# Weight groups narrowed in stages, one stage a step, in a two-MLP kernel on one core

## The chip, the cores and the metric

The kernel runs on one core of one Trainium2 chip. The metric is the device time of one execution in microseconds; the median of several executions is given. The engines are called as the profile calls them: PE (TensorE, matrix products; PEld is its loading of weights), DVE (VectorE), ACT (ScalarE), POOL (GpSimd) and SP (SyncE, which issues the transfers here).

## The reference

A Fourier transform over sequence and features, its real part, and then two MLPs one after the other, with float32 results:

```python
def _attn_ref(x):                      # x: 2 x 3008 x 256
    X = np.fft.fft(x, axis=1)
    X = np.fft.fft(X, axis=2)
    return X.real.astype(np.float32)

def _moe_ref(x, w_in, w_out):          # 6016 x 256, 256 x 2048, 2048 x 256
    r = np.maximum(x @ w_in, 0.0)
    return ((r * r) @ w_out).astype(np.float32)

def _moe2_ref(x, w_in, w_out):
    h = x @ w_in
    g = h * (1.0 / (1.0 + np.exp(-1.702 * h)))
    return (g @ w_out).astype(np.float32)
```

The weights come as float64. They reach the chip as pairs of 32-bit words, and the kernel makes float32 of them itself.

## The kernel before

**Products.** Every float32 operand of a product is held as a high part of a rounded type and a low part, the rest. A product of two operands is three matrix products: high with high, high with low, low with high. The tokens are cut into eight blocks of 376 or 378 columns (two halves each, which the symmetry of the transform ties together).

**Steps.** The first MLP is one loop of 128 steps (L684 to L737), numbered from 0. A step takes one block j and one slice f of 128 hidden features. PE makes the hidden product into a pair of banks of PSUM (`front1`, L453 to L455; two such pairs exist, so PE is at most two steps ahead of DVE), then the output product of the step that lies four steps back (`back`, L468, `LAG = 4`). DVE evacuates the hidden product with three instructions (L710, L712, L713), the last of which frees the second bank. ACT does relu, square and the high part (L719, L720, L722); in the steps of the set `SV` DVE does relu and square in one instruction (L717). POOL subtracts for the low part (L76, tile gl); in the steps of `VSTEPS` DVE does. Where a block ends, `store` (L573) copies the two output sums from PSUM, one on ACT and one on DVE (L581), and sends them to DRAM.

**Background work.** Everything else that the two MLPs need is a generator of items, an item being mostly one instruction. `PLAN` (L33) gives for each generator the first step, the rate in items per step, and the step by which it must be done. `background(i)` (L558) takes the items that fall on step i. The scheduler of the language orders each engine's instructions by the order in which they are written and by when it expects them to be ready; from step 18 on (`THROTTLE`) a DVE or ACT instruction of the background stands behind that step's last DVE or ACT instruction. A generator that isn't done at its due step is run to its end there.

**Narrowing.** `narrow` (L162) makes float32 of a group of weights, 1024 per partition, in six items: Abs of the high words on ACT (L169), a clamp of the result (L170) and a shift (L171) on DVE, the scaled low words (on ACT, L175, for the groups in the set `RA`, else on DVE, L177), the merging of sign and top bit (L178) and the addition (L180), both on DVE. L171 reads L170's result, L178 that of L175 or L177, L180 those of L171 and L178. Then the group is widened into a high part (a copy on ACT, L203 or L241) and a low part (a subtraction, L76, tile w or w2i, on POOL or DVE by the table `LOW`). The input groups of the first MLP have a sum and a masked difference between the two (L200, L201), those of the second four differences on POOL (L233), two copies and two subtractions, each in two instructions.

**Where it runs.** A group is named by MLP, kind (0 input, 1 output) and number. "conv" narrows groups (0,0,1), (0,1,1), (0,0,2), (0,1,2), (0,0,3), (0,1,3) from step 3 on; the scratch tiles of the kinds differ. "w2a" narrows (1,0,2), (1,1,2), (1,0,3) from step 55, "w2b" (1,1,3), (1,0,0), (1,1,0), (1,0,1), (1,1,1) from step 85; all groups of these two share one scratch tile, so the Abs of a group waits for the last subtraction of the group before. `then` loads the next group's words by SP once `narrow` is done; `park` (L211) sends four of the widened w2 groups to DRAM until they are needed. "odd1" (`odd_k`, L398) prepares two blocks of the second batch from step 79: two sums, then for each block `split_eo` (high part on ACT, low part on POOL for the first and DVE for the second) and `nyquist`, a small matrix product (L418, L419) that reads both parts.

The second MLP follows the loop, in an order written out by hand. It doesn't concern the change.

Of the kernel before, what the change touches and what calls it, by code (L numbers as in the profile page):

```python
# [12 lines left out]
AF = mybir.ActivationFunctionType  # L13
# [19 lines left out]
PLAN = {  # L33
# [4 lines left out]
}  # L38
# [25 lines left out]
def spectral_two_mlps_kernel(  # L64
# [7 lines left out]
    def f32(ap):  # L72
        return ap.bitcast(F32)
# [88 lines left out]
    def narrow(raw, ue, key=None):  # L162
# [5 lines left out]

        yield lambda: A.activation(out=u, in_=f32(hw), func=AF.Abs)  # L169
        yield lambda: V.tensor_scalar(out=u, in0=u, scalar1=LEAST, scalar2=TOP, op0=ALU.max, op1=ALU.min)  # L170
        yield lambda: V.tensor_scalar(out=uu, in0=uu, scalar1=3, scalar2=0x3FFFFFF8,  # L171
                                      op0=ALU.logical_shift_left, op1=ALU.bitwise_and)

        if key in RA:
            yield lambda: A.activation(out=eu, in_=lw, func=AF.Copy, scale=2.0 ** -29)  # L175
        else:
            yield lambda: V.tensor_scalar(out=eu, in0=lw, scalar1=2.0 ** -29, scalar2=None, op0=ALU.mult)  # L177
# [4 lines left out]
    def temp(pool, tag="xt"):  # L182
        return pool.tile([P, 2, 1024], F32, tag=tag, name="ue")
# [3 lines left out]
    def widen(mlp, kind, g, temps, dest, then=None, tag="xt"):  # L187
# [17 lines left out]
        if mlp and (kind, g) in PARKED:  # L205
            park((mlp, kind, g), w)
        weights[mlp, kind, g] = w

    parked = {}
# [188 lines left out]
    def odd_k(b, pool, tag="xt", later=0):  # L398
# [26 lines left out]
        yield lambda: sums(1)  # L425
        yield lambda: split_eo(b, 2, e2)
        yield lambda: nyquist(2)
        while at_step[0] < later:
            yield lambda: None
        yield lambda: split_eo(b, 3, e3)  # L430
        yield lambda: nyquist(3)

# [95 lines left out]
    def at(name, job):  # L528
        i, rate, end = PLAN[name]
        plan.setdefault(i, []).append((name, rate, job))  # L530
        if end is not None:
# [5 lines left out]
    at("conv", lambda: chain(*(  # L537
        widen(0, k, g, xp, (winp, wq)[k], tag=("t", "x0")[k],
              then=(lambda k=k, g=g: load_w(0, k, g + 1)) if g < 3 else None)
        for g in (1, 2, 3) for k in range(2))))  # L540
# [101 lines left out]
    def w2_jobs(lo, hi):  # L642
        for i in range(lo, hi):
# [3 lines left out]
            if k == 0:  # L647
                yield from widen_in(g, temp(cv2), dest, then=then)
            else:
                yield from widen(1, 1, g, cv2, dest, then=then)  # L650

# [347 lines left out]
```

## Time and profile before

| | |
|---|---|
| median of 3 runs | 1035.78 us (1034.14 to 1037.46) |
| the profiled execution | 1034.19 us, span of its instructions 1032.1 us |
| PE busy | 987.3 us, 96% of the span |
| DVE, ACT, POOL busy | 823.0, 616.4, 351.0 us |
| mean granted clock of PE | 0.985 |
| the 128 steps of the first MLP | from about 35 to 520 us |
| PE busy from 524 us to the end | 503.5 of 508.1 us |

The profile is one execution. Busy times of a stretch come from the table by windows; an instruction's start and duration from the timeline, where the bracket at the end of a line is the time for which its engine was idle before it and what ended that. A granted clock of 1.00 is 2.4 GHz, 0.50 is 1.2 GHz. The busy time of PE is that at whichever clock was granted.

### The profile page before, as it was taken

The numbers are of one execution on the slowest core, as the hardware profiler recorded it, in microseconds if no ns is written. First come the engines' busy times: TensorE is split into PE (matmuls) and PEld (weight loads), VectorE is DVE, ScalarE is ACT, GpSimd is POOL, SyncE is SP. The second block draws the span as 40 slices with busy tenths as digits, with TensorE's granted clock in tenths as the row PEclk, the third lists the DMA queues.
The fourth block names the chain that finished last, engine by engine and source line by source line (L and its number), as shares of the span: only waits on it lengthen the run. The fifth ranks groups of instructions, "written<-read, shape, count | busy, mean of one in ns | idle before, by whom it ended". The sixth has DMA issues, their size and how long they took to land.

```text
span 1032.1 us, 14239 instructions
## 1 busy us (share of the span) xinstructions
PE 987.3 (96%) x5582; PEld 951.4 (92%) x5582; DVE 823.0 (80%) x1089; ACT 616.4 (60%) x764; POOL 351.0 (34%) x216
## 2 busy tenths in 40 slices
PE   8988988999989999898989999999999999999998
PEld 8578987898989799898989999999999999999997
DVE  7997889885877579677668888888988888888875
ACT  2576576775688578787754554554555455454443
POOL 2457474534567546776715210102020020200000
PEclk9898999999999999999999999999999999999999
DMA  7532212101142112101342100000100000000000
GB/s 286 209 108 80 72 71 82 72 31 53 42 140 85 72 67 88 70 32 61 114 138 94 61 31 30 30 32 7 54 1 30 31 31 31 1 31 1 31 1 30
DMA packets 22914, 65.22 MB, mean 63 GB/s; under 512 B 1856, under 2 KB 14272, under 8 KB 19648
## 3 DMA queue, kind: packets, MB, share of 16 engines
q1 hardware_dynamic: 22848, 64.32, 17.5%
q8 instruction: 43, 0.70, 0.3%
q14 instruction: 23, 0.19, 0.1%
HBM read 43.13 MB, written 21.19 MB: 62 GB/s over the span
## 4 chain that ended last, share of the span: by engine, by line
PE 53%; DVE 3%; ACT 2%; issue 1%; POOL 0%; DVEq 0%; ACTq 0%
PE psb L779 25%; PE psc L763 22%; PE psb L468 4%; ACT h L720 1%; ACT h L719 1%; PE psa L453 1%; PE psa L455 0%; PE psa L454 0%; DVE ue L177 0%; DVE gl L76 0%; DVE ue L178 0%; DVE ue L170 0%; ACT gh L722 0%; DVE yc L76 0%; DVE h L712 0%
## 5 line engine op out<-in xcount | busy, mean ns | idle before, releaser
L76 POOL TENSOR_TENSOR gl<-h,gh 128x752 fp32r<-128x752 f32 (+1 forms) x113 | 215.3, 1913 | 170.8 <-ACT gh L722 153.3
L468 PE MATMUL psb<-gh,w 128*128 128x376 f32 (+1 forms) x1024 | 244.4, 341 | 4.0 <-ACT o L581 3.4
L779 PE MATMUL psb<-gh,w 128*128 128x376 f32 (+1 forms) x1024 | 237.7, 334 | 0.0
L468 PEld LDWEIGHTS psb<-gh,w 128*128 128x128 f32 x1024 | 187.2, 193 | 5.5 <-ACT o L581 4.5
L779 PEld LDWEIGHTS psb<-gh,w 128*128 128x128 f32 x1024 | 182.9, 188 | 0.0
L719 ACT ACTIVATE h<-h 128x752 f32<-128x752 f32 (+1 forms) x116 | 96.5, 832 | 79.5 <-DVE h L713 77.3
L844 ACT ACTIVATE g<-c 128x1128 f32<-128x1128 f32 (+1 forms) x64 | 73.8, 1152 | 99.7 <-DVE c L842 99.7
L468 PE MATMUL psb<-gl,w 128*128 128x376 f32 (+1 forms) x512 | 133.1, 341 | 0.0
L779 PE MATMUL psb<-gl,w 128*128 128x376 f32 (+1 forms) x512 | 129.9, 335 | 0.4 <-DVE gl L76 0.3
L722 ACT CAST gh<-h 128x752 fp32r<-128x752 f32 (+1 forms) x128 | 105.3, 822 | 22.7 <-DVE h L717 19.5
L453 PE MATMUL psa<-eo,w 128*128 128x376 f32 (+1 forms) x256 | 90.3, 354 | 25.1 <-DVE h L713 15.1
L76 DVE TENSOR_TENSOR gl<-g,gh 128x1504 fp32r<-128x1504 f32 (+1 forms) x64 | 111.7, 1745 | 1.6 <-ACT gh L824 1.6
L824 ACT CAST gh<-g 128x1504 fp32r<-128x1504 f32 (+1 forms) x64 | 93.1, 1454 | 31.8 <-DVE g L815 31.8
L710 DVE SCALAR_TENSOR_TENSOR p<-n,w1n_t,psa 128x376 f32<-128x376 f32 (+1 forms) x128 | 75.9, 599 | 45.0 <-PE psa L455 44.9
L615 POOL TENSOR_TENSOR ue<-raw 128x376 f32<-128x376 f32 (+1 forms) x16 | 19.5, 1237 | 270.6 <-DVE ya L76 270.5
L720 ACT ACTIVATE h<-h 128x752 f32<-128x752 f32 (+1 forms) x116 | 96.7, 835 | 3.3
L468 PEld LDWEIGHTS psb<-gl,w 128*128 128x128 f32 x512 | 95.5, 194 | 0.0
L779 PEld LDWEIGHTS psb<-gl,w 128*128 128x128 f32 x512 | 92.1, 188 | 1.0 <-DVE gl L76 1.0
L815 DVE TENSOR_TENSOR g<-g,c 128x1128 f32<-128x1128 f32 (+1 forms) x64 | 89.5, 1399 | 1.2 <-ACT g L844 1.2
L841 DVE TENSOR_TENSOR g<-g,psc 128x376 f32<-128x376 f32 (+1 forms) x64 | 35.0, 546 | 68.9 <-ACT g L840 68.9
L454 PE MATMUL psa<-eo,w 128*128 128x376 f32 (+1 forms) x256 | 86.2, 337 | 0.0
L455 PE MATMUL psa<-eo,w 128*128 128x376 f32 (+1 forms) x256 | 86.1, 337 | 0.0
(138 smaller groups left out, 1627.8 us busy)
## 6 DMA issues: line engine op xcount, KB each, us to landing
ydram<-o SPq DMA_DIRECT2D x18, 376.0 KB, 2.8
xt<-in_x SPq DMA_DIRECT2D x5, 1024.0 KB, 7.0
cst<-in_dfts SPq DMA_DIRECT2D x8, 570.0 KB, 6.0
raw<-ydram SPq DMA_DIRECT2D x6, 752.0 KB, 4.6
out<-o SPq DMA_DIRECT2D x11, 376.0 KB, 3.1
raw<-in_w1i SPq DMA_DIRECT2D x4, 1024.0 KB, 5.8
raw<-in_w1o SPq DMA_DIRECT2D x4, 1024.0 KB, 7.3
raw<-in_w2i SPq DMA_DIRECT2D x4, 1024.0 KB, 4.9
```

The source lines that it names most:

```text
L76: eng.tensor_tensor(out=o, in0=a, in1=f32(b), op=ALU.subtract)
L453: T.matmul(o, lhsT=w[:, 0, fs], rhs=t[:, par, 0, 0:wd], start=True, stop=False)
L454: T.matmul(o, lhsT=w[:, 0, fs], rhs=t[:, par, 1, 0:wd], start=False, stop=False)
L455: T.matmul(o, lhsT=w[:, 1, fs], rhs=t[:, par, 0, 0:wd], start=False, stop=True)
L468: T.matmul(acc[j][ec][:, s, 0:wd], lhsT=w[:, hl, e0:e0 + P], rhs=(gh, gl)[gi][:, s, 0:wd], start=(first and hl == 0 and gi == 0), stop=(la ...
L719: A.activation(out=hv, in_=hv, func=AF.Relu)
L720: A.activation(out=hv, in_=hv, func=AF.Square)
L722: last_a = A.copy(gh[:, :, 0:wd], hv)
L763: T.matmul(bank, lhsT=w[:, hl, slot * P:(slot + 1) * P], rhs=t[:, yl, i], start=(first and hl == 0 and yl == 0), stop=(hl == 1), skip_grou ...
L779: T.matmul(o[:, s, 0:wd], lhsT=w[:, hl, e0:e0 + P], rhs=g[:, 2 * i + s, 0:wd], start=(f == 0 and hl == 0 and g is gh), stop=(f == 15 and h ...
L815: V.tensor_tensor(out=g[:, 1:4, 0:pw], in0=g[:, 1:4, 0:pw], in1=c[:, :, 0:pw], op=ALU.mult)
L824: A.copy(gh[:, :, 0:pw], g[:, :, 0:pw])
```

## The change

The items of a group are handed out in stages. `staged` draws several items of a group's generator at once: for a group in `RA` two, two and two of `narrow` (Abs and scaled low words on ACT; clamp and shift on DVE; merging and addition on DVE), for another one, three and two (Abs; clamp, shift and scaled low words on DVE; merging and addition). Then follow, for an output group, the copy and the subtraction, one a stage; for an input group of the first MLP, sum and masked difference, the copy, the subtraction; for one of the second, the four differences, the first copy, the first subtraction with the second copy, the second subtraction. For the groups in `RA`, except the very first one, the scaled low words come right behind Abs. The rates go from 2, 1.6 and 1.7 items to 1.2, 1 and 1.04 stages a step; first and due steps stay. In w2, an empty item follows a group whose low part POOL makes, unless it is the last of its generator. In "odd1" an empty item stands between `split_eo` and `nyquist`.

```diff
-    "out0": (0, 12, 3), "even01": (0, 1, 4), "odd0": (1, 1, 48), "conv": (3, 2, 36),
+    "out0": (0, 12, 3), "even01": (0, 1, 4), "odd0": (1, 1, 48), "conv": (3, 1.2, 36),
...
-    "cst3": (66, 4, 67), "odd1": (79, 1, 88), "w2a": (55, 1.6, 78), "w2b": (85, 1.7, 117), "y0": (117, 1, 128),
+    "cst3": (66, 4, 67), "odd1": (79, 1, 88), "w2a": (55, 1, 78), "w2b": (85, 1.04, 117), "y0": (117, 1, 128),
...
         yield lambda: A.activation(out=u, in_=f32(hw), func=AF.Abs)
+        early = key in RA and key != (0, 0, 0)
+        if early:
+            yield lambda: A.activation(out=eu, in_=lw, func=AF.Copy, scale=2.0 ** -29)
...
-        if key in RA:
+        if early:
+            pass
+        elif key in RA:
             yield lambda: A.activation(out=eu, in_=lw, func=AF.Copy, scale=2.0 ** -29)
...
+    def staged(key, gen):
+
+        mlp, kind, _ = key
+        first = (2, 2, 2) if key in RA else (1, 3, 2)
+        for k in first + ((1,) if kind else (4, 1, 2) if mlp else (2, 1)):
+            yield lambda: run(gen, k)
+        yield lambda: run(gen)
...
         yield lambda: split_eo(b, 2, e2)
+        yield from [lambda: None] * b
         yield lambda: nyquist(2)
...
         yield lambda: split_eo(b, 3, e3)
+        yield from [lambda: None] * b
         yield lambda: nyquist(3)
...
-        widen(0, k, g, xp, (winp, wq)[k], tag=("t", "x0")[k],
-              then=(lambda k=k, g=g: load_w(0, k, g + 1)) if g < 3 else None)
+        staged((0, k, g), widen(0, k, g, xp, (winp, wq)[k], tag=("t", "x0")[k],
+                                then=(lambda k=k, g=g: load_w(0, k, g + 1)) if g < 3 else None))
...
             if k == 0:
-                yield from widen_in(g, temp(cv2), dest, then=then)
+                yield from staged((1, 0, g), widen_in(g, temp(cv2), dest, then=then))
             else:
-                yield from widen(1, 1, g, cv2, dest, then=then)
+                yield from staged((1, 1, g), widen(1, 1, g, cv2, dest, then=then))
+            if LOW[1, k, g] == "G" and i < hi - 1:
+                yield lambda: None
```

## Rows read from the trace of the kernel before

**Rows 1.** Windows: stretch, its length, busy us (instructions) by engine, clock, DMA share, GB/s.

```profile
62.00:160.00 98.00, 88.05 (x470) 84.41 (x469) 82.61 (x109) 66.08 (x81) 57.21 (x29) 0.95 0.20 67
...
266.00:326.00 60.00, 55.12 (x312) 53.29 (x312) 47.48 (x67) 44.64 (x57) 39.42 (x26) 1.00 0.33 114
...
360.00:374.00 14.00, 11.51 (x56) 10.89 (x56) 8.39 (x12) 10.04 (x14) 5.98 (x4) 0.88 0.15 57
...
419.00:484.00 65.00, 57.56 (x311) 55.71 (x310) 51.03 (x71) 51.93 (x66) 45.23 (x29) 0.95 0.16 54
```

**Rows 2.** Windows of the five stretches at half clock: the first, the sum.

```profile
90.00:96.70 6.70, 6.22 (x19) 5.72 (x20) 5.23 (x9) 6.48 (x9) 3.62 (x2) 0.50 0.32 117
...
sum 20.20, PE 19.25 PEld 18.76 DVE 16.37 ACT 14.64 POOL 10.31; mean PE 3.85 PEld 3.75 DVE 3.27 ACT 2.93 POOL 2.06
```

**Rows 3.** Timeline (start, duration, instruction) of an undisturbed step: DVE, then PE.

```profile
455.44 0.61 DVE L710 SCALAR_TENSOR_TENSOR p<-n,w1n_t,psa 128x376 f32<-128x376 f32 x1 [1.36 <-PE psa L455]
...
456.64 0.54 DVE L713 TENSOR_TENSOR h<-p,psa 128x376 f32<-128x376 f32 x1
...
458.34 0.33 PE L453 MATMUL psa<-eo,w 128*128 128x376 f32 x1
...
461.45 0.33 PE L453 MATMUL psa<-eo,w 128*128 128x376 f32 x1
```

**Rows 4.** Groups by line, 60 to 520: busy us, mean ns, idle before.

```profile
L180 DVE CUSTOM_DVE_ANT_0 ue<-ue 128x2048 uint16<-128x2048 uint16 x12 | 19.1, 1592 | 0.0
L178 DVE SCALAR_TENSOR_TENSOR ue<-raw,ue 128x1024 uint32<-128x1024 uint32 x12 | 19.0, 1586 | 1.4 <-ACT ue L175 1.3
L170 DVE TENSOR_SCALAR ue<-ue 128x1024 f32<-128x1024 f32 x12 | 17.3, 1438 | 6.6 <-ACT ue L169 6.6
L177 DVE TENSOR_SCALAR ue<-raw 128x1024 uint32<-128x1024 uint32 x7 | 13.8, 1974 | 6.1 <-POOL w2i L76 4.8 <-POOL w L76 1.2
L171 DVE TENSOR_SCALAR ue<-ue 128x1024 uint32<-128x1024 uint32 x12 | 13.0, 1087 | 0.1
L581 DVE COPY o<-psb 128x752 f32<-128x752 f32 x8 | 7.5, 934 | 0.1
...
L233 POOL TENSOR_TENSOR ue<-ue 128x256 f32<-128x256 f32 x16 | 11.8, 740 | 4.6 <-DVE ue L180 3.6
```

**Rows 5.** Timeline of ACT, DVE and PE in w2a, at one group's start.

```profile
294.76 1.16 ACT L169 ACTIVATE ue<-raw 128x1024 f32<-128x1024 f32 x1 [0.76 <-POOL w2i L76]
...
295.95 1.14 DVE L170 TENSOR_SCALAR ue<-ue 128x1024 f32<-128x1024 f32 x1 [4.27 <-ACT ue L169]
...
302.64 0.44 PE L453 MATMUL psa<-eo,w 128*128 128x378 f32 x1 [2.67 <-DVE p L710]
```

**Rows 6.** Timeline of ACT in w2b, in front of a store's copy.

```profile
420.82 1.12 ACT L169 ACTIVATE ue<-raw 128x1024 f32<-128x1024 f32 x1 [3.07 <-POOL w2i L76]
```

**Rows 7.** Timeline of DVE: the narrowing of the first group of w2b.

```profile
376.90 1.43 DVE L170 TENSOR_SCALAR ue<-ue 128x1024 f32<-128x1024 f32 x1 [0.19 <-ACT ue L169]
378.36 0.69 DVE L171 TENSOR_SCALAR ue<-ue 128x1024 uint32<-128x1024 uint32 x1
...
380.58 1.31 DVE L177 TENSOR_SCALAR ue<-raw 128x1024 uint32<-128x1024 uint32 x1
381.92 1.23 DVE L178 SCALAR_TENSOR_TENSOR ue<-raw,ue 128x1024 uint32<-128x1024 uint32 x1
...
384.72 1.53 DVE L180 CUSTOM_DVE_ANT_0 ue<-ue 128x2048 uint16<-128x2048 uint16 x1
```

**Rows 8.** Timeline of PE at the first nyquist product of odd1.

```profile
362.64 0.44 PE L419 MATMUL psa<-eo,sel_t 128*128 128x376 f32 x1 [1.94 <-POOL eo L76]
```

**Rows 9.** Timeline of DVE: single instructions of other groups, in w2b and w2a.

```profile
464.63 2.29 DVE L177 TENSOR_SCALAR ue<-raw 128x1024 uint32<-128x1024 uint32 x1 [1.24 <-POOL w2i L76]
...
469.59 2.06 DVE L171 TENSOR_SCALAR ue<-ue 128x1024 uint32<-128x1024 uint32 x1
...
273.52 2.75 DVE L180 CUSTOM_DVE_ANT_0 ue<-ue 128x2048 uint16<-128x2048 uint16 x1
```

## The prediction

> **What bounds the kernel now.** I read the windows by stage first. In the stretches where weights are narrowed and in the one of the two nyquist products PE is not busy throughout: 98.0 - 88.05 = 9.9 us are idle in 62 to 160 (the chain "conv"), 60.0 - 55.12 = 4.9 in 266 to 326 ("w2a"), 14.0 - 11.51 = 2.5 in 360 to 374 (the tail of "odd1") and 65.0 - 57.56 = 7.4 in 419 to 484 (most of "w2b") [rows 1]. That is 24.8 us. Just behind such idle time five stretches, 20.2 us together, run at a granted clock of 0.50, so at 1.2 and not 2.4 GHz; work there takes twice its time, so 10.1 us go with them (6.7/2 in conv, and four of about 3.4/2: one in conv, one in odd1, two in w2b); the first of the five and the sum over them stand in [rows 2]. So some 35 us at most can come from this change, which touches nothing else.
>
> Next, an undisturbed step [rows 3]. PE starts the second half of its hidden product at 458.34 and the next at 461.45: a step is 3.11 us. DVE spends 455.44 to 457.18 = 1.74 us on its own three instructions, and PE needs the two banks that the last of them frees only at 461.45, so DVE may be 461.45 - 457.18 = 4.3 us late without PE noticing. Hence the rule that I use: lateness grows by DVE's extra work in a step less 1.4 us (3.11 - 1.74); what exceeds 4.3 becomes PE idle time.
>
> Third, why DVE is later than that. An engine takes its instructions in their issued order, so a wait holds what is queued behind it. At 294.76 ACT's Abs of a new group has had to wait for POOL, which was still subtracting for the group before; DVE stands 4.27 us idle for this Abs, with the next step's evacuation queued behind, and PE then loses 2.67 us [rows 5]. At 420.82 the same wait of ACT, 3.07 us, has queued behind it the copy that frees the output sums, on which PE waits [rows 6]. Over 60 to 520, DVE waited 6.6 us for Abs (before L170) and 6.1 us for POOL (before L177) [rows 4].
>
> **The change part by part.** The instructions of a group are the same; their steps differ. Before, rates of 2, 1.6 and 1.7 single instructions a step put Abs and the DVE instruction that reads it often into the same step. Now one stage goes out at a step: Abs (with the scaled low word, where ACT makes it) in one, DVE's clamp and shift (and its own scaled low word) in the next, mask-and-or plus add in the third. Before a group whose predecessor's last subtraction is on POOL, an empty item is put in w2.
>
> *w2a (steps 55 to 75).* Three groups. The waits of rows 5 go: POOL's last subtraction of a group is issued two steps, 6.2 us, before the next Abs, and Abs a step before its reader. Late next is DVE itself: three instructions in one step, two in the next. What that costs is almost seen before: the group in 376 to 387 follows a quiet stretch and has three (1.43 + 0.69 + 1.31 = 3.4 us) and then two (1.23 + 1.53 = 2.8) between the evacuations of successive steps, and PE lost nothing [rows 7]. By the rule: 3.4 - 1.4 = 2.0, then 2.0 + 2.8 - 1.4 = 3.4, under 4.3. With the means of all groups (1.44 + 1.09 + 1.97 = 4.5 and 1.59 + 1.59 = 3.2 [rows 4]) it is 3.1 and 4.9, so 0.6 lost. I take 0.3 a group, midway, since rows 7 lacks only the POOL work of a neighbour. w2a: 4.9 - 0.9 = 4.0 gained (3.1 to 4.9).
>
> *w2b (steps 85 to 115).* Five groups. The first is that of rows 7 itself; one more is split 2 and 2, with ACT taking a part, and stays under 4.3. Two more behave as in w2a. But at a rate of 1.04 step 99 gets two stages: all five DVE instructions, and this is also a step that stores, 0.93 more [rows 4]: 6.2 + 0.9 - 1.4 = 5.7 to 7.7 + 0.9 - 1.4 = 7.2, so 1.4 to 2.9 lost. I take 2.3, and 0.9 for the three others: 7.4 - 3.2 = 4.2 gained (2.7 to 6.0). The wait of rows 6 goes, as the POOL subtraction is issued at 96 and not 97, the Abs still at 98.
>
> *odd1.* PE waited 1.94 us for POOL's low part of the input [rows 8], and 2.5 in the whole window [rows 1]. The product is now issued a step, 3.11 us, later; its result is needed 13 steps later at the earliest. 2.5 gained (1.9 to 2.5). It holds a bank pair a step later as well, at a step in which DVE has no narrowing before its own three instructions; if it had, up to 1 us would come back.
>
> *conv (steps 3 to 29).* Neighbouring groups use different buffers here, so Abs has no POOL wait to lose; DVE waited at most 6.6 - 4.3 = 2.3 us for Abs here [rows 4, 5]. Before step 18 nothing ties this work to its step, so the placing is loose. The DVE work of a group is 1.44, 1.09 and 1.59 + 1.59 = 3.2 in three steps before: by the rule 1.8 late at most. At 1.2 items a step every fifth step now gets two stages, and at steps 4 and 9 these are all four DVE instructions: 5.7 - 1.4 = 4.3 late, 2.5 more than before. With other DVE work beside them (the relu that it does at step 9) nothing of the margin is left, and the bound is 2 x 2.5 = 5.0 lost. The other bound is that all 9.9 go. I take 1.0 gained, somewhat under half of the wait for Abs, which is the one part with a row.
>
> *At no cost.* The four POOL differences of a w2 group, before spread over two to three steps, are issued in one: 4 x 0.74 = 3.0 us [rows 4]. POOL is busy 45.2 of 65 us there [rows 1], and its low part is multiplied four steps, 12.4 us, after it is begun; were this cover gone, a step would wait some 3 us. ACT's two instructions of a stage delay its relus, with the same cover. Weight loads go out up to two steps earlier; a parked group's store leaves the SP queue at once rather than with the next item, and the only transfers behind it are loads needed several steps later. If one of them were late, PE would wait for weights, some us once.
>
> *Clock.* The stretch of odd1 and one of the two of w2b should stay at full clock: 2 x 1.7 = 3.4 gained (0 to 10.1).
>
> **Sum.** 4.0 + 4.2 + 2.5 + 1.0 + 3.4 = 15.1 us. The profiled execution took 1034.2 us, 2.1 more than its span of 1032.1, and 1034.2 - 15.1 = 1019.1. The median of the runs shown is 1035.8, 1.6 above it, which would make 1020.7; I say 1020.
>
> **Rivals.**
> *Cleaner than that.* Conv loses its waits too and all half-clock time goes: 9.9 - 1.0 in conv, 10.1 - 3.4 of the clock and 1.8 of w2 (its six groups at 0) beyond the forecast, 17.4. That is 1003. For it: at the durations of rows 7 four DVE instructions (4.9) leave DVE 3.5 late, under 4.3. Against: steps 4 and 9 carry more DVE work than any did.
>
> *A burst takes the wait's place.* Six groups at 0.6 and step 99 at 2.9 make 6.5 in place of 12.3; with odd1 and its clock (4.2), 4 lost in conv and a half-clock stretch more (1.7) the gain is 5.8 + 4.2 - 4.0 - 1.7 = 4.3: 1032, with a reach to 1036. For it: the means. Against: rows 7.
>
> *Slower: DVE and POOL block each other.* A DVE instruction on weights takes 0.69 us alone [rows 7] and 2.0 to 2.8 while POOL works, and each of a series can meet a POOL instruction anew: 2.29, 2.06, 2.75 [rows 9]. Packed stages make such series the rule. At 2.2 each for three and 2.7 for two, a group gives 6.6 - 1.4 = 5.2, of which 0.9 lost, then 4.3 + 5.4 - 1.4 = 8.3, 4.0 lost: 4.9 a group. From three blocked groups on (4.6 more each than counted), with conv at its bound (6.0 more than counted), the gain is gone: 13.8 + 6.0 = 19.8 against 15.1. With four and one half-clock stretch more it is 1020 + 18.4 + 6.0 + 1.7 = 1046. For it: rows 9, both placings have five such instructions a group. Against: in rows 9 POOL had a backlog of weight subtractions just before, which the empty item now keeps two steps away.
> The Trainium skill (SBUF — State Buffer, section "SBUF: two separate sides") gives that rival a rule: VectorE and GpSimd share one port pair, whoever starts first holds it for its whole instruction, and the other is fully blocked. The stretched durations agree with it; by it alone every series beside POOL work would be stretched, and the time would be this rival's 1046.
>
> **How the numbers follow.** Forecast (1010 to 1029) 0.60; cleaner 0.11; burst 0.17; blocking 0.12. The range leaves out the blocking rival and the lower part of the cleaner one: 1008 to 1036. A measurement of this kernel tells about 0.3%, 3.1 us, from no change: faster means under 1032.7. That is 0.60 + 0.11 and a third of the burst case, 0.77; within, the rest of it, 0.11; slower, the blocking case, 0.12.
>
> **What would show it.** Right: PE idle in the windows of w2a and w2b together under 6 us instead of 12.3; no wait of ACT's Abs for POOL's weight subtractions, no wait of L170 for Abs; no PE wait for the low part in odd1; a PE wait left near the store at step 99 and near steps 9 and 19. Wrong: L170, L177 or L180 at 2 us or more on the mean with waits of PE for DVE behind each group; or PE waits for POOL's low part or for weights, which no step of mine has.

## The result, and the profile after

The changed kernel takes 1021.93 us (median of 4 runs, 1021.64 to 1024.11) against 1034.96 us for the kernel before (4 runs, 1033.23 to 1037.46). The ratio is 0.9886, 95% interval [0.9866, 0.9905]. The profiled execution took 1022.03 us, its span is 1020.2 and its mean granted clock 0.990. The span is 11.9 us shorter. The same lines have new numbers: L170 is now L173, L171 is L174, L177 is L182, L178 is L183, L180 is L185, L581 is L596; L169 and L76 stay.

Windows of the changed kernel first (stretch, length, busy us and instructions by engine, clock, DMA share, GB/s). They lie earlier than those of [rows 1], since the kernel is ahead by then: conv, w2a, the tail of odd1, all of w2b (before, PE idles nowhere in w2b ahead of 419, so its 7.4 us are also those of all of w2b).

```profile
60.00:157.00 97.00, 88.25 (x493) 84.14 (x493) 83.06 (x116) 67.92 (x85) 55.40 (x29) 1.00 0.24 82
258.00:320.00 62.00, 61.17 (x351) 60.08 (x350) 48.64 (x76) 51.11 (x67) 47.92 (x32) 1.00 0.30 111
345.00:359.00 14.00, 13.81 (x80) 13.33 (x79) 10.04 (x15) 13.39 (x19) 7.22 (x4) 1.00 0.15 57
370.00:470.00 100.00, 93.75 (x518) 91.22 (x518) 80.12 (x113) 79.46 (x104) 70.59 (x44) 0.97 0.17 59
```

PE idle, before and after: conv 9.9 and 8.75, w2a 4.9 and 0.8, odd1 2.5 and 0.2, w2b 7.4 and 6.25. The last column but two is the clock: conv had 0.95 and has 1.00. Both its half-clock stretches of 6.7 and 3.4 us [rows 2] are gone though its idle time hardly fell, and the one in odd1 is gone as well. What is left in this part of the kernel are two others, again as windows:

```profile
413.30:420.10 6.80, 6.06 (x19) 6.07 (x20) 3.74 (x9) 5.96 (x8) 3.34 (x2) 0.50 0.32 133
478.20:481.60 3.40, 3.40 (x11) 3.40 (x12) 0.98 (x2) 2.26 (x3) 3.40 (x3) 0.50 0.00 0
```

So the saving has these parts: conv 1.2 of idle time and 5.1 of clock, w2a 4.1, odd1 2.3 and 1.7 of clock, w2b 1.2 and nothing of clock (6.8 us at half clock before and after); against them, 2.2 of idle time and 1.7 of clock are new at 476. These come to 11.7 us, beside 11.9 us of the span. They fit only to about 1 us: PE is 0.7 us ahead already at the first nyquist product (62.20 us, before 62.91), and that start differs as much between executions (62.15 us in odd1_only, 62.93 in y0_item, both below).

What the engines waited for, groups by line from 60 to 510 (busy us, mean ns, idle before):

```profile
L183 DVE SCALAR_TENSOR_TENSOR ue<-raw,ue 128x1024 uint32<-128x1024 uint32 x12 | 19.7, 1642 | 0.0
L185 DVE CUSTOM_DVE_ANT_0 ue<-ue 128x2048 uint16<-128x2048 uint16 x12 | 19.1, 1596 | 0.0
L173 DVE TENSOR_SCALAR ue<-ue 128x1024 f32<-128x1024 f32 x12 | 16.1, 1340 | 5.9 <-ACT ue L169 5.8
L169 ACT ACTIVATE ue<-raw 128x1024 f32<-128x1024 f32 x11 | 12.6, 1144 | 1.6 <-DMA raw<-in_w1o 1.6
L182 DVE TENSOR_SCALAR ue<-raw 128x1024 uint32<-128x1024 uint32 x7 | 8.5, 1221 | 0.0
```

Against [rows 4]: DVE's wait for POOL ahead of the scaled word went from 6.1 us to 0 and that instruction from 1974 to 1221 ns on the mean; Abs no longer waits for POOL's weights. The wait of DVE's clamp for Abs is still 5.8 us where it was 6.6, but in waits of at most 2.2 us where one of 4.27 stood [rows 5]. That one has more than one part. This is what ACT did in the kernel before, just ahead of the Abs of [rows 5]:

```profile
293.17 0.82 ACT L722 CAST gh<-h 128x756 fp32r<-128x756 f32 x1
```

DVE stood idle from 291.68 us. Until 293.99 ACT worked on relu, square and high part of that step; then it waited 0.76 us for POOL, and Abs took 1.16. So most of the 4.27 us came from Abs standing in the step of its reader, behind that step's own work on ACT, and the smaller part from POOL. In w2a of the changed kernel it looks like this (timeline: start, duration, instruction, idle before; ACT, DVE, PE):

```profile
281.66 1.14 ACT L169 ACTIVATE ue<-raw 128x1024 f32<-128x1024 f32 x1
...
282.83 1.44 DVE L173 TENSOR_SCALAR ue<-ue 128x1024 f32<-128x1024 f32 x1 [1.07 <-ACT ue L169]
...
292.58 0.44 PE L468 MATMUL psa<-eo,w 128*128 128x378 f32 x1 [0.35 <-DVE h L730]
```

DVE waits 1.07 us, which is no more than Abs itself takes, and PE loses 0.35 where it lost 2.67 [rows 5].

Step 99 is what remains of w2b (timeline of DVE and POOL, then PE):

```profile
401.91 2.32 DVE L182 TENSOR_SCALAR ue<-raw 128x1024 uint32<-128x1024 uint32 x1
404.15 2.31 DVE L173 TENSOR_SCALAR ue<-ue 128x1024 f32<-128x1024 f32 x1
406.38 0.93 DVE L596 COPY o<-psb 128x752 f32<-128x752 f32 x1
407.23 1.43 DVE L174 TENSOR_SCALAR ue<-ue 128x1024 uint32<-128x1024 uint32 x1
408.58 2.83 DVE L183 SCALAR_TENSOR_TENSOR ue<-raw,ue 128x1024 uint32<-128x1024 uint32 x1
...
401.84 8.49 POOL L76 TENSOR_TENSOR gl<-h,gh 128x752 fp32r<-128x752 f32 x4
...
407.37 0.61 PE L483 MATMUL psb<-gh,w 128*128 128x376 f32 x2 [1.49 <-DVE o L596]
...
411.99 0.44 PE L468 MATMUL psa<-eo,w 128*128 128x376 f32 x1 [1.26 <-DVE p L727]
...
414.04 0.68 PE L468 MATMUL psa<-eo,w 128*128 128x376 f32 x1 [1.26 <-DVE h L730]
```

There is no wait on DVE in it: 9.8 us of work (2.32 + 2.31 + 0.93 + 1.43 + 2.83) stand between two evacuations, and PE loses 4.0 us there; 6.8 us at half clock follow.

The new stall at 476, POOL and PE:

```profile
472.96 3.46 POOL L620 TENSOR_TENSOR raw<-raw,ue 128x1512 f32<-128x1512 f32 x1 [2.72 <-DMA ue<-ydram]
476.37 3.53 POOL L76 TENSOR_TENSOR gl<-h,gh 128x752 fp32r<-128x752 f32 x2
...
478.20 1.00 PE L483 MATMUL psb<-gl,w 128*128 128x376 f32 x2 [2.23 <-POOL gl L76]
```

POOL waits 2.72 us for a transfer and then adds for 3.46 us, while the subtraction for which PE waits stands behind. The kernel before did its subtraction first.

### The profile page after: what moved, and what is told of

It is laid out like the page before. It is cut to its first block, busy times and chain, and to the rows that moved or that the text cites. A ratio compares the mean times of both kernels' runs of the same rounds, so it can differ in the third digit from the quotient of the medians.

```text
span 1020.2 us, 14245 instructions
## 1 busy us (share of the span) xinstructions
PE 983.7 (96%) x5582; PEld 948.6 (93%) x5582; DVE 816.6 (80%) x1089; ACT 612.9 (60%) x764; POOL 354.6 (35%) x216
## 4 chain that ended last, share of the span: by engine, by line
PE 69%; DVE 16%; ACT 7%; issue 5%; POOL 1%; DMA 0%; DVEq 0%; ACTq 0%; POOLq 0%
PE psb L796 24%; PE psc L780 21%; PE psb L483 13%; PE psa L468 2%; PE psa L367 2%; ACT h L736 2%; PE psa L469 2%; PE psa L470 2%; DVE h L730 2%; DVE p L727 2%; DVE h L729 2%; ACT h L737 2%; DVE ue L183 1%; DVE gl L76 1%; PE psa L284 1%
## 5 line engine op out<-in xcount | busy, mean ns | idle before, releaser
L76 POOL TENSOR_TENSOR gl<-h,gh 128x752 fp32r<-128x752 f32 (+1 forms) x113 | 218.5, 1944 | 157.9 <-ACT gh L739 135.7
L76 DVE TENSOR_TENSOR gl<-g,gh 128x1504 fp32r<-128x1504 f32 (+1 forms) x64 | 111.8, 1747 | 1.6 <-ACT gh L841 1.6
L468 PE MATMUL psa<-eo,w 128*128 128x376 f32 (+1 forms) x256 | 90.5, 355 | 16.9 <-DVE h L730 11.6
```

Of the source, the lines that this page charges most:

```text
L76: eng.tensor_tensor(out=o, in0=a, in1=f32(b), op=ALU.subtract)
L468: T.matmul(o, lhsT=w[:, 0, fs], rhs=t[:, par, 0, 0:wd], start=True, stop=False)
```

## The experiments

Medians are to be held against 1021.9 us (ratio 0.9886 [0.9866, 0.9905]) for the changed kernel, and 1034.2 to 1035.9 us for the kernel before, which was run again beside each; the ratios are to that.

**One of the three edits at a time.** odd1_only is the kernel before with the two empty items of `odd_k` alone:

```diff
         yield lambda: split_eo(b, 2, e2)
+        yield from [lambda: None] * b
```

> The kernel before with one edit: the empty item between splitting and the nyquist product in the second batch. Theory (PE waits there only for the low part, which a step covers): the 2.5 us of idle time at that place and the half-clock stretch behind it (1.7) go, 4.2 us less than before, about 1031. Rival (the product is only moved into a place where it waits for DVE, or the idle time comes back at the next store): within 1 us of before, 1034 to 1036.

1032.63 us (10 runs), ratio 0.9986 [0.9974, 0.9999], between the theory's 1031 and the rival's range. At the place itself all came as expected: PE's waits of 1.94 [rows 8] and 0.55 us are down to 0.18, and the half clock behind them is gone, together 4 us. In the profiled execution the rest of the kernel gave more than half of it back: 0.35 and 0.55 us of idle time at 394 and 398 and 1.4 at 511 are new, and the switch to the second MLP at 517 waits 3.7 us where it waited 2.8.

conv_old is the changed kernel with conv as before:

```diff
-    "out0": (0, 12, 3), "even01": (0, 1, 4), "odd0": (1, 1, 48), "conv": (3, 1.2, 36),
+    "out0": (0, 12, 3), "even01": (0, 1, 4), "odd0": (1, 1, 48), "conv": (3, 2, 36),
...
-        early = key in RA and key != (0, 0, 0)
+        early = key in RA and key[0] == 1
...
-        staged((0, k, g), widen(0, k, g, xp, (winp, wq)[k], tag=("t", "x0")[k],
-                                then=(lambda k=k, g=g: load_w(0, k, g + 1)) if g < 3 else None))
+        widen(0, k, g, xp, (winp, wq)[k], tag=("t", "x0")[k],
+              then=(lambda k=k, g=g: load_w(0, k, g + 1)) if g < 3 else None)
```

> The changed kernel, with the chain conv as before (2 single items a step, the scaled low words in their old place). By the prediction, conv is worth 1.0 us: 1023. By the two traces, 1.2 us of idle time and two half-clock stretches (5.1 us) are gone from conv's windows: 1028, with the half-clock stretches at 90 and 145 us back.

1028.61 us, ratio 0.9947 [0.9926, 0.9968]: conv is worth 6.7 us (1028.61 - 1021.93), what the traces had said and not the prediction's 1.0. In its windows the clock tells more than the idle time (97.00 - 87.43 = 9.6 against 8.75):

```profile
60.00:157.00 97.00, 87.43 (x467) 83.72 (x466) 81.76 (x109) 65.17 (x81) 59.17 (x29) 0.95 0.21 73
89.20:96.00 6.80, 6.16 (x19) 5.48 (x19) 5.32 (x9) 6.64 (x9) 3.62 (x2) 0.50 0.32 116
143.80:147.20 3.40, 3.40 (x13) 3.40 (x12) 2.87 (x6) 2.42 (x4) 1.46 (x1) 0.50 0.03 5
```

The first stretch at half clock follows this wait (timeline, PE of conv_old); the longest wait of the changed kernel in conv, under it, has none behind it:

```profile
88.07 0.44 PE L468 MATMUL psa<-eo,w 128*128 128x376 f32 x1 [2.01 <-DVE h L730]
```

```profile
153.89 0.44 PE L468 MATMUL psa<-eo,w 128*128 128x378 f32 x1 [1.39 <-DVE h L730]
```

The second stretch follows two waits of 1.36 and 0.62 us, at 142 and 143, both shorter than that. So the length of a wait doesn't tell which has a stretch behind it. But the stretches of conv aren't chance: all four kernels with the old pairing there (before, odd1_only, conv_old and old_pairs) have both, and the nine that pair the instructions there as the change does run at full clock from 60 to 240 us.

old_pairs keeps the new pace of conv (1.2) but not the place of ACT's scaled word, which in these groups again comes behind the shift, so that the stages are Abs with clamp, shift with scaled word, merge with add:

```diff
-        early = key in RA and key != (0, 0, 0)
+        early = key in RA and key[0] == 1
```

> The changed kernel, with the scaled low words of conv's groups back in their old place in the order: conv keeps its two items a stage and its 1.2 stages a step, but the pairs are now Abs with the clamp that reads it, and the shift with the scaled low words, so a stage holds what its own stage makes on the other engine. Theory (what matters is that DVE doesn't wait for ACT within a stage): conv's idle time grows by 1 to 4 us and at least one half-clock stretch comes back, 1024 to 1029. Rival (conv's gain is one of pace, 1.2 stages in place of 2 items a step, wherever the pairs are cut): 1021 to 1023.

1026.89 us (8 runs, 1022.6 to 1029.63), ratio 0.9927 [0.9904, 0.9950]. The two half-clock stretches in conv are back, 6.8 us at 90 and 3.4 at 151, each behind a long wait (2.0 and 3.05 us). The medians part by 5.0 us from the changed kernel, though the intervals just touch; of that 1 us may be step 99's, where this execution lost 4.95 us and the changed kernel 4.0. So it is the pairing, and not the slower pace, that gives conv most of its gain. The theory's reason, a wait for ACT within the stage, is not what the traces show: from 60 to 160 us DVE waits 1.1 us for Abs in conv_old, 1.6 in old_pairs and 1.3 in the changed kernel. Ahead of the wait of 2.0 us stand these two (timeline of DVE in conv_old; old_pairs and the kernel before have them alike):

```profile
81.73 2.58 DVE L734 SCALAR_TENSOR_TENSOR h<-h 128x752 f32<-128x752 f32 x1
...
84.75 2.36 DVE L173 TENSOR_SCALAR ue<-ue 128x1024 f32<-128x1024 f32 x1
```

The first is the relu that DVE does in some steps, the second the clamp of the next group, whose Abs was done more than 20 us before. Both meet a row of subtractions on POOL; the relu takes 0.94 us at 82 in the changed kernel. There the same clamp comes 25 us later, when POOL is idle:

```profile
109.83 0.69 DVE L173 TENSOR_SCALAR ue<-ue 128x1024 f32<-128x1024 f32 x1
```

So the pairing acted by the place at which the clamp came, and by what it met there.

**Which distance counts in w2.** Between POOL's last subtraction of a group and the first DVE instruction of the next group the changed kernel has three steps: subtraction, empty, Abs, DVE. Five kernels move Abs, or take steps away.

joined puts Abs into the step of its readers and keeps them three steps behind POOL (in conv too):

```diff
-        first = (2, 2, 2) if key in RA else (1, 3, 2)
-        for k in first + ((1,) if kind else (4, 1, 2) if mlp else (2, 1)):
+        yield lambda: None
+        for k in (4, 2) + ((1,) if kind else (4, 1, 2) if mlp else (2, 1)):
```

> The changed kernel, but each group's ACT instructions and the clamp and shift that read them (and the scaled low word where DVE makes it) come in one stage, one step later than Abs stands now; an empty stage takes the freed step, so every other stage keeps its step. Theory (a DVE instruction that waits for ACT in its own step holds the evacuations behind it): the clamp waits about 2 us in most of the 13 staged groups, PE loses 5 to 9 us of the gain, 1027 to 1031. Rival (only the amount of DVE work per step and its meeting with POOL matter, waits for Abs fill time that DVE would idle anyway): 1021 to 1024.

1026.68 us, ratio 0.9929 [0.9906, 0.9953], just under the theory's range, but not by its mechanism: the clamp waits 3.0 us for Abs between 258 and 470, in four waits of at most 1.1, where it waits 4.5 us in the changed kernel. What grew is the time of DVE's own instructions (the table below).

abs_at_pool has the empty item behind Abs, not ahead of it, so Abs stands right behind POOL:

```diff
+        if after_pool:
+            yield lambda: run(gen, first[0])
+            yield lambda: None
+            first = first[1:]
...
+            after_pool = i > lo and LOW[(1, *order[i - 1])] == "G"
...
-            if LOW[1, k, g] == "G" and i < hi - 1:
-                yield lambda: None
```

> The changed kernel, with the empty item of the second MLP's groups moved from ahead of Abs to behind it: Abs is issued one step earlier, right behind POOL's last subtraction of the group before; every other stage keeps its step. Theory (ACT's wait for POOL holds relus and the store's copy): ACT waits 1 to 3 us for POOL in five groups, and PE loses 3 to 5 us of the gain, 1025 to 1027. Rival (ACT has enough room, and only waits of DVE reach PE): 1021 to 1023, with ACT's waits for POOL in the trace but no PE idle time behind them.

1020.22 us, ratio 0.9871 [0.9846, 0.9897]: the rival's time, and not apart from that of the changed kernel, since the intervals overlap. Waits of ACT in 258 to 470 (us in total, times, longest), then the window of w2a:

```profile
ACT ue L169 <- POOL w2i L76: 2.6, 2, 1.9
```

```profile
258.00:320.00 62.00, 61.90 (x359) 61.58 (x358) 47.65 (x74) 52.45 (x69) 50.39 (x33) 1.00 0.31 113
```

PE loses 0.1 us in the whole of w2a. But this doesn't say that ACT's waits for POOL are free: both are in w2b. Behind the longer one stands the copy of a store on ACT, and PE waits for that copy (timeline of ACT and PE):

```profile
399.29 1.15 ACT L169 ACTIVATE ue<-raw 128x1024 f32<-128x1024 f32 x1 [1.91 <-POOL w2i L76]
...
403.61 0.61 PE L487 MATMUL psb<-gh,w 128*128 128x376 f32 x2 [1.43 <-ACT o L600]
```

That is the chain of [rows 6] again, in small, and what the theory had. In all_bound (below) ACT waits 2.56 us for POOL at 397, the copy stands six instructions behind that Abs and not three, and PE waits for no copy of ACT.

neither puts Abs and its readers into one step right behind POOL and two empty steps behind them:

```diff
+        if after_pool:
+            yield lambda: run(gen, 4)
+            yield lambda: run(gen, 2)
+            yield lambda: None
+            yield lambda: None
+            first = ()
```

> The changed kernel, but in the second MLP a group that follows a POOL subtraction gets neither distance: Abs and its readers on DVE come in one stage, in the step right behind that subtraction; two empty items behind the narrowing keep all later stages in their steps. With only one of the two distances taken away before, little came back in these groups. Theory (each distance alone keeps DVE from standing still for Abs; without both it waits for POOL by way of Abs, as before the change): DVE waits 1 to 4 us at such groups, w2a's idle time goes from 0.8 to 3 to 5 us, 1025 to 1029. Rival (the number of DVE instructions per step, which is not higher here, or the even pace made the gain): 1021 to 1023.

1029.54 us (10 runs), ratio 0.9963 [0.9945, 0.9981], 0.5 us above the theory's range. But the wait is not the one that I had in mind (waits of DVE, 258 to 470):

```profile
DVE ue L182 <- POOL w2i L76: 11.1, 3, 6.1
```

DVE hardly waits for Abs (0.3 us); it waits for POOL itself. The scaled word goes first on DVE, though it is written third, and it is written over the tile that POOL is still reading for the group before.

no_empty is the changed kernel without the empty items: subtraction, Abs, DVE.

> The changed kernel without the empty items: Abs stands in a step of its own right behind POOL's last subtraction of the group before, its readers one step later, with nothing between. Everything of the second weights comes up to four steps earlier. Theory 1, one step between Abs and its reader is what matters, and a wait of ACT for POOL of up to 3 us is covered: 1020 to 1024, under 1.5 us of PE idle in the first part of the second weights. Rival, one of the two distances must be two steps, as in the changed kernel and in abs_at_pool: ACT is 2 to 3 us late, the reader waits for Abs again, 1025 to 1030, with 2 us or more idle there.

1029.52 us, ratio 0.9950 [0.9932, 0.9968]: the rival's time, but again by the other wait (timeline of POOL, DVE and PE):

```profile
402.70 2.27 POOL L76 TENSOR_TENSOR w2i<-ue,w2i 128x512 fp32r<-128x512 f32 x2
...
405.00 2.29 DVE L182 TENSOR_SCALAR ue<-raw 128x1024 uint32<-128x1024 uint32 x1 [3.06 <-POOL w2i L76]
...
412.23 0.68 PE L468 MATMUL psa<-eo,w 128*128 128x376 f32 x1 [5.37 <-DVE p L725]
```

all_three was to join the three improvements found until then (abs_at_pool, step99 and y0_item, both below), and doesn't: the list of stages is made ahead, and the first stage behind POOL read its length from the shortened tuple. It issued Abs, clamp and shift together right behind POOL, then an empty step, then the other three.

> The changed kernel with the empty item behind Abs instead of ahead of it (no PE idle in the first part of the second weights when tried alone), no step with two stages in their second part, and one more item between the load and POOL's add for the y0 product. Theory: the three act in different places, so the gains add: 1.7 + 3.2 + 0.5 below 1021.9, so 1015 to 1018. Rival: part of each returns as a stall later, since DVE and POOL hand on their lateness: 1018 to 1021.

1031.63 us (12 runs), ratio 0.9973 [0.9961, 0.9986]. Here the scaled word is three steps behind POOL and the clamp one step. DVE waits 9.7 us for Abs in 258 to 470, in four waits; the longest, in w2b (timeline of ACT, DVE and PE):

```profile
407.09 1.14 ACT L169 ACTIVATE ue<-raw 128x1024 f32<-128x1024 f32 x1 [2.54 <-POOL w2i L76]
...
408.27 1.12 DVE L173 TENSOR_SCALAR ue<-ue 128x1024 f32<-128x1024 f32 x1 [4.35 <-ACT ue L169]
...
415.64 0.68 PE L472 MATMUL psa<-eo,w 128*128 128x376 f32 x1 [2.28 <-DVE p L737]
```

POOL holds Abs, Abs holds the clamp, the clamp holds the evacuation, and PE waits 1.15, 2.28 and 2.13 us. In w2a, where PE loses 6.8 us, POOL holds no Abs; DVE's longest wait for one there is 2.1 us.

Side by side, in us (w2a is 254 to 324, before 258 to 328; w2b is 324 to 490, before 374 to 500; "narrowing" is the busy time of DVE's fifteen narrowing instructions for the three groups of w2a; five is the next experiment):

| kernel | steps from POOL to DVE's scaled word | steps from Abs to its reader | w2a: DVE waits for POOL; for Abs (longest) | w2a: narrowing | w2a: PE idle | w2b: DVE waits for POOL; for Abs | w2b: PE waits for DVE and ACT | median |
|---|---|---|---|---|---|---|---|---|
| before | 2 to 3 | 0 | 1.2; 5.3 (4.3) | 22.8 | 4.9 | 4.8; 0.2 | 7.5 | 1034.2 to 1035.9 |
| after | 3 | 1 | 0; 3.7 (2.2) | 19.1 | 0.8 | 0; 0.8 | 6.4 | 1021.9 |
| abs_at_pool | 3 | 2 | 0; 1.6 (1.1) | 19.5 | 0.1 | 0; 2.4 | 6.5 | 1020.2 |
| joined | 3 | 0 | 0; 1.5 (0.9) | 23.8 | 2.8 | 0.8; 1.6 | 6.0 | 1026.7 |
| no_empty | 2 | 1 | 0; 0.9 (0.5) | 22.0 | 4.1 | 5.6; 0.3 | 12.0 | 1029.5 |
| neither | 1 | 0 | 2.5; 0.8 (0.5) | 22.0 | 3.3 | 9.6; 0 | 11.6 | 1029.5 |
| all_three | 3, clamp 1 | 0 | 0; 3.1 (2.1) | 21.8 | 6.8 | 0; 7.2 | 8.9 | 1031.6 |
| five | 3 | 1 | 0; 0 | 24.6 | 5.3 | 0; 1.4 | 11.9 | 1033.8 |

In w2b the waits of DVE go with the loss in no_empty, neither and all_three: it waits 5.6 to 9.6 us for POOL or for Abs, and PE waits 9 to 12 us and not 6. In w2a they don't: joined has less of them than the changed kernel and loses 2.0 us more. What goes with the loss there is the time of the narrowing instructions themselves, 19 us in the two kernels that lose under 1 us and 22 to 25 in all others. In no_empty an evacuation in w2a waits for POOL besides, which still reads the buffer for a low part (timeline of DVE):

```profile
297.12 0.55 DVE L727 TENSOR_TENSOR h<-p,psa 128x378 f32<-128x378 f32 x1 [2.60 <-POOL gl L76]
```

So that the distances count is shown. Whether in w2a they act by DVE's waits or by what its instructions meet on POOL is not separated, since each of these edits moves both.

**How much DVE work goes into one step.** five keeps both distances, the pace and the number of stages, and issues the five DVE instructions of a group in one step and none in the next:

```diff
-        first = (2, 2, 2) if key in RA else (1, 3, 2)
+        first = (2, 2, 2) if key in RA else (1, 5, 0)
```

> Every second-weight group but the one that ACT helps with issues all its five DVE instructions in one step and none in the next; Abs stays a step ahead, the number of stages and the pace stay. This tests the lateness rule of the prediction with a size of its own. With the means after the change the five are 1.34 + 1.10 + 1.22 + 1.64 + 1.60 = 6.9 us; less 1.4 and less the margin of 4.3 that is 1.2 lost a group, with the short durations of an undisturbed group (6.2) 0.5: for seven groups 3.5 to 8.4, against about 1 that the groups lose now, and perhaps a half-clock stretch of 1.7: theory 1024 to 1031, with 1.5 to 3.6 us of PE idle in 258 to 320 instead of 0.8. Rival 1, the rule is too mild, as at step 99, where it said 2.3 and 4.0 came: four a group, 1040 and more, 8 us idle there. Rival 2, the margin is larger than the rule says, and only the waits for another engine counted: 1021 to 1023, idle there below 1.2.

1033.80 us (10 runs), ratio 0.9998 [0.9985, 1.0012]: as much as the whole change gained is gone, more than the theory allowed, though less than in rival 1. In w2a PE is idle 5.3 us. DVE's narrowing waits nowhere for POOL and 1.4 us for Abs. What grew are the instructions (groups of DVE in w2a):

```profile
L183 DVE SCALAR_TENSOR_TENSOR ue<-raw,ue 128x1024 uint32<-128x1024 uint32 x3 | 6.7, 2234 | 0.1
L173 DVE TENSOR_SCALAR ue<-ue 128x1024 f32<-128x1024 f32 x3 | 5.3, 1764 | 0.0
L174 DVE TENSOR_SCALAR ue<-ue 128x1024 uint32<-128x1024 uint32 x3 | 4.5, 1509 | 0.0
L182 DVE TENSOR_SCALAR ue<-raw 128x1024 uint32<-128x1024 uint32 x2 | 3.8, 1903 | 0.0
L185 DVE CUSTOM_DVE_ANT_0 ue<-ue 128x2048 uint16<-128x2048 uint16 x3 | 3.6, 1212 | 0.0
```

The means add to 8.6 us a group; in the changed kernel the same five add to 6.5 in the same window. Why, a timeline of DVE and POOL in five shows:

```profile
282.45 1.23 DVE L183 SCALAR_TENSOR_TENSOR ue<-raw,ue 128x1024 uint32<-128x1024 uint32 x1
283.59 2.31 DVE L173 TENSOR_SCALAR ue<-ue 128x1024 f32<-128x1024 f32 x1
...
280.05 1.81 POOL L76 TENSOR_TENSOR gl<-h,gh 128x752 fp32r<-128x752 f32 x1 [0.51 <-ACT gh L739]
282.51 2.84 POOL L76 TENSOR_TENSOR gl<-h,gh 128x752 fp32r<-128x752 f32 x1 [0.65 <-DVE ue L182]
```

DVE started first, at 282.45, and took its usual 1.23 us; POOL, begun 0.06 us later, took 2.84 where it takes 1.81, 1.0 longer. The clamp, begun at 283.59, ends 0.55 us after POOL does, and took 2.31. Each one's time is about its own and what was left of the other's. The Trainium skill (SBUF — State Buffer, section "SBUF: two separate sides") names an exclusive lock on a port pair that the two share, held for a whole instruction; these rows agree with it.

step99 takes the one double stage out of w2b (rate 1, and the last subtraction of the first group issued together with the next Abs, so that the chain isn't longer):

```diff
-    "cst3": (66, 4, 67), "odd1": (79, 1, 88), "w2a": (55, 1, 78), "w2b": (85, 1.04, 117), "y0": (117, 1, 128),
+    "cst3": (66, 4, 67), "odd1": (79, 1, 88), "w2a": (55, 1, 78), "w2b": (85, 1, 117), "y0": (117, 1, 128),
...
+            if i == 3:
+                kept = stages.pop()
+            elif i == 4:
+                stages[0] = (lambda a=kept, c=stages[0]: (a(), c()))
```

> The changed kernel, with w2b at exactly one stage a step (31 stages from step 85 to 115): the last subtraction of its first group, on DVE, and the Abs of the next come in one stage, and so no step has two stages; step 99 has the merge and the addition alone beside its store. Theory (five DVE instructions and a store's copy in one step make DVE later than the 4.3 us that PE bears): the 4.0 us of idle time at 405 to 414 and the half-clock stretch behind it (3.4) go, less 1 for two instructions that remain there: 1015 to 1018. Rival (PE waits there for the store's copies anyway, or the lateness moves elsewhere): 1020 to 1023.

1018.77 us, ratio 0.9862 [0.9838, 0.9886], against 0.9886 for the changed kernel: 3.2 us less by the medians, just short of what was expected; the intervals overlap. The half clock at 413 is gone, the idle time only in part, from 4.0 to 3.0 us. The first three DVE instructions of that group still take 2.30, 2.33 and 2.15 us, beside POOL's backlog.

**The stall at 476.** y0_item puts one more empty item between the load and POOL's add:

```diff
-            yield lambda: None
+            yield from [lambda: None] * (1 if j else 2)
```

> The changed kernel, with one more empty item between the load of the first partial sum for the second MLP and POOL's addition that reads it, steps 117 to 119. Theory (POOL stands 2.7 us before that addition for the load, and the low parts behind it come late): the 2.2 us in which PE waits for a low part at 476 and the half-clock stretch behind it (1.7) go, 1018 to 1020. Rival (everything behind is a step later, so the second MLP's start waits as much longer): 1021 to 1023.

1021.42 us, ratio 0.9894 [0.9866, 0.9922]: no change, as the rival had it, though not for its reason, since the second MLP's start waits 2.88 us at 508 where it waited 3.18. The wait of 2.23 us became two of 0.71 and 0.70. The add still waits 2.71 us for its transfer, so one item was not enough to take that wait off POOL's queue. The half clock at 478 went, and another one of 3.4 us appeared at 462, behind waits of 0.33, 0.59 and 0.36 us; the changed kernel has the same three there (0.32, 0.58, 0.35) and no half clock. Nor does the one at 478 belong to its wait: in abs_at_pool PE waits 2.24 us at the same place, and behind that the window shows full clock:

```profile
474.00:480.00 6.00, 4.46 (x26) 4.46 (x27) 2.61 (x5) 2.69 (x5) 5.92 (x6) 1.00 0.00 0
```

So of what is new at 476 only the 2.2 us of idle time are the change's; the 1.7 us of clock come and go between executions.

**Together.** all_bound is all_three with the length bound where it is written, so abs_at_pool, step99 and y0_item at once.

> The kernel that all_three was meant to be. There the first stage behind a POOL subtraction read its length late and took three instructions, so Abs and its two readers stood in one step right behind POOL, with an empty step after them: the placing that the change removes. Here that stage is Abs alone, an empty step follows, then clamp, shift and scaled word; no step with two stages in the second part, and one more item ahead of POOL's add for the y0 product. Theory: the parts act in different places, the gains add, 1015 to 1018, and PE idle in 258 to 320 returns from 6.7 to below 1. Rival: lateness is handed on, 1018 to 1021.

1019.12 us (5 runs, 1016.34 to 1019.63), ratio 0.9838 [0.9815, 0.9861]: the lowest ratio of all, and the rival's range. Its windows of 420 to 500:

```profile
420.00:470.00 50.00, 47.41 (x269) 45.84 (x269) 39.72 (x57) 41.42 (x55) 34.47 (x23) 1.00 0.14 48
470.00:500.00 30.00, 27.00 (x154) 26.09 (x154) 17.01 (x28) 22.58 (x29) 24.99 (x16) 1.00 0.27 101
```

w2a loses 0.1 us, but 2.6 and 3.0 us are idle in these two, where the changed kernel loses 1.25 and 2.2. Its interval overlaps those of step99 and abs_at_pool, so it isn't shown to be better than either; against the changed kernel the intervals do not meet.

## Why the prediction was right, and where its parts were not

The time, 1022 us against 1020 in a range of 1008 to 1036, was right. The sum behind it, 15.1 us where 13.0 came, hides three terms that were off by 3 to 6 us each, in both directions; that they nearly cancel is luck. Two of the signs that the prediction named for being right did not come: PE idles 7.1 us in w2a and w2b together (0.8 + 6.25), not under 6, and the clamp still waits for Abs.

*w2a, right in size.* 4.0 forecast with 0.9 left, 4.1 measured with 0.8 left. The reason was half right. The prediction put the 4.27 us of [rows 5] down to POOL, by way of ACT; POOL's part of it is 0.76 us, and most of the rest is Abs standing in the step of its reader. It also took the waits for the whole loss, where DVE's narrowing instructions for the three groups took 22.8 us before and 19.1 after; which of the two carried how much of the gain stays open. That the changed kernel would have no wait for Abs at all was wrong: 5.8 us are left, none of them longer than 2.2 us, and in w2a, where 3.7 of them are, PE loses 0.8 us.

*w2b, wrong in size.* 4.2 forecast, 1.2 measured. The place was named, step 99 with its two stages and its store; the term was 2.3 and measured 4.0, the other groups lose 2.2 us where 0.9 was counted, and of the 3.4 us that the clock costs in w2b, half of which the sum counted as won, none was. Mis-sized at step 99 was the duration: I took 6.2 to 7.7 us for the five instructions. Four of them take 8.9 here (2.32 + 2.31 + 1.43 + 2.83), beside a POOL that works through four subtractions without a pause. The rule itself held: with the measured durations it gives 9.8 - 1.4 - 4.3 = 4.1. It is rough all the same: in five it gives 8.6 - 1.4 - 4.3 = 2.9 a group in w2a, where 5.3/3 = 1.8 was lost.

*odd1, right at its place.* 2.5 and 1.7 forecast, 2.3 and 1.7 measured there. Alone it gives 1.6 us of that by the medians; the rest comes back later. A saving in one stage was booked in full. Why in particular the waits at 394 and 511 grow was not settled.

*conv, wrong.* 1.0 forecast, 6.7 measured by conv_old. The idle time came out as sized (1.2), but by luck: the term was half of DVE's wait for Abs, and that wait is as long as before (1.1 and 1.3 us). What failed is the step on the clock, which gave its 3.4 us to odd1 and w2b and none to conv, where both stretches went. What the prediction had no term for is the relu and the clamp of DVE that POOL stretched at 82 to 87. The bursts that it feared at steps 4 and 9 cost little: from 34 to 60 us PE has the same waits in both kernels, and from 60 to 85 us it idles 2.8 us where it idled 2.3, with DVE's four instructions of a group one at a time between the evacuations.

*At no cost, one thing overlooked.* The y0 work, which the diff doesn't touch, lost 2.2 us at 476, and 1.7 of clock in the profiled execution. The prediction named a wait for POOL's low part as something that no step of it has, and that is what came. Every queue behind a stage that ends earlier is part of the change.

*The rivals.* Burst in the wait's place, 1032: five shows that such bursts are real (1033.8 us; that the numbers agree is chance, since five keeps what conv and odd1 gain), and the stages of three and two avoid them except at step 99. DVE and POOL blocking each other, 1046: the stretch is real as well, but the change did not make more of it. Over all groups the means hardly changed (clamp 1.34 us, merge 1.64, addition 1.60 against 1.44, 1.59, 1.59 [rows 4]), that of the scaled word fell from 1.97 to 1.22, and in conv one case of it went. The cleaner case failed on step 99, on 476 and on conv, where 8.75 us of idle time are left.

## What to carry to other kernels

Where background work shares in-order queues with a loop, ask of each of its instructions how many steps lie between it and the other engine's instruction that it needs, the last reader of its tile included, and what it will run beside. A wait matters on the engine that holds the bound engine's buffers next: on DVE here, and on ACT where the copy of a store stands close behind (1.43 us in abs_at_pool). Placing such work without waits gains nothing if it then comes in one piece: two pieces of up to 3 instructions fitted here, one of 5 cost as much as the whole change had gained. And don't count the clock by the sum of idle time or by its longest wait: 1.2 us less idle time brought 5.1 us of clock in conv, and the same wait of 2.2 us at 476 cost 1.7 us of clock in one kernel and none in another.

## What the runs showed of the hardware

- DVE and POOL lengthen each other's instructions by about what was left of the one that started first: POOL 2.84 instead of 1.81 us beside a DVE instruction of 1.23, DVE's clamp 2.31 behind it, where it takes 0.69 undisturbed (109.83 in the changed kernel), and four POOL subtractions 8.49 us in a row beside DVE's series, 2.12 each.
- Whether a half-clock stretch follows an idle time of PE isn't told by its length in these runs: 2.01 us (conv_old, at 88) and 1.94 [rows 8] had one behind them, 2.48 us (step99, at 402) and 2.67 [rows 5] had none. Nor is it the same from one execution to the next at the same place with the same waits: 2.23 us at 478 (the changed kernel) had 3.4 us at half clock behind it, 2.24 at 475 (abs_at_pool) none. So one such wait is uncertain by the 1.7 us that a stretch of 3.4 costs, which is part of why single variants differ by what their idle times don't explain.
